# Attention decode, forward and backward: V transposed as fp32 pairs, and O by wide matmuls

## The chip, the cores and the metric

The kernel runs on one core of a Trainium2 chip. The metric is the device time of one execution in microseconds; smaller is better. The kernel before takes 668.13 us (median of three, 667.49 to 668.91). Its profiled execution spans 667.0 us.

## The reference

Softmax attention with one query row for each of 32 heads, 8192 keys and a head width of 128, all in bf16, and its gradients for a given gradient of the output:

```python
B, H, Sq, Skv, Dh = 1, 32, 1, 8192, 128

def _fwd_reference(q, k, v):
    scale = q.shape[-1] ** -0.5
    scores = jnp.einsum('bhqd,bhkd->bhqk', q, k) * scale
    attn = _softmax(scores, axis=-1)
    return jnp.einsum('bhqk,bhkd->bhqd', attn, v)

def reference(q, k, v, grad_out):
    ...
    _out, _vjp = jax.vjp(_f, q, k, v)
    _grads = _vjp(grad_out)
    return (_out0, *[jnp.asarray(_g) for _g in _grads])
```

With p the softmax row of a head and do its output gradient, a head needs o = p V; dp = V do; ds = p (dp - o·do) times the scale; dq = ds K; and the outer products dK = ds q and dV = p do. So K and V (2 MiB each) are read once per head, and dK and dV (2 MiB each) are written: 8.39 MB a head, 268 MB in all.

## The kernel before

A head's K or V lies in SBUF as [128 partitions, 64 slots, 128 columns]. The products o and dq contract over the keys, which lie in the partitions, so they take the tensor as it is. The scores of K and dp contract over the head width, so they need it transposed. K is transposed on VectorE in 32 x 32 blocks of fp32 words, each a pair of bf16. V is transposed on TensorE, 16 slots at a time, and copied out of PSUM by ScalarE:

```python
    def v_transposes(h, c):
        T_ps = psT.tile([P, CH, P], BF16, tag="T", name="T_ps")
        for i in range(CH):                                    # CH = 16
            nc.tensor.transpose(T_ps[:, i, :], Vt[h][:, c * CH + i, :], ident[:])   # L168
        X = tpool.tile([P, CH, P], BF16, tag="XT", name="XT_sb")
        nc.scalar.copy(X.rearrange("p c s -> p (c s)").bitcast(F32),                # L170
                       T_ps.rearrange("p c s -> p (c s)").bitcast(F32))
        XV[h, c] = X

    def v_scores(h, c):
        X = XV.pop((h, c))
        ...
        for i in range(CH):
            n = c * CH + i
            nc.tensor.matmul(st[h]["dp"][:, n:n + 1], lhsT=X[:, i, :], rhs=doT[:, h:h + 1],   # L180
                             start=True, stop=True, skip_group_check=True)

    def contract(Xt, rep, out_col, first=0, last=NT):          # NT = 64
        for n in range(first, last):
            nc.tensor.matmul(out_col, lhsT=Xt[:, n, :], rhs=rep[:, n, 0:1],                   # L185
                             start=(n == 0), stop=(n == NT - 1), skip_group_check=True)
```

`contract` makes the slot of K or V the stationary operand (128 columns loaded) and one column of weights the moving one. The loop runs one head's scores and softmax between the parts of the previous head's backward pass, in the order written (scheduling by the tool is off):

```python
    for h in range(H + 1):
        p_ = h - 1
        if h < H:
            for u in range(NCH):
                k_blocks(h, u)            # VectorE, L133: K transposed
            k_scores(h)                   # 64 matmuls of four columns, L145
            if 0 < h < H - 1:
                load_v(h + 1)             # L81
        if h > 0:
            ds_of(p_)                     # reads o.do through pdt, L216
            outer(p_, "dk", 0)            # VectorE, L195; its output leaves at L203
            dq_of(p_, 0)                  # contract over K
        ...                               # s_mask, s_swap: scores put into place, L161
        if h > 0:
            dq_of(p_, 1)
            outer(p_, "dk", 1)
        if 0 < h and h + 2 < H:
            load_k(h + 2)                 # L75
        ...                               # maximum (L255), q and do broadcast (L207), exp, sum (L268)
        x["p"] = small.tile([P, NT, R], BF16, tag="prep", name="p_rep")
        nc.scalar.activation(x["p"][:], ..., ACT.Copy, scale=rinv[:])       # R = 4 copies of p, L277
        ...
        v_transposes(h, 0)
        contract(Vt[h], x["p"], x["m"][:, 2:3])
        nc.scalar.copy(o_all[:, h:h + 1], x["m"][:, 2:3])
        v_transposes(h, 1)
        nc.tensor.matmul(x["m"][:, 1:2], lhsT=do_f[:, h:h + 1].to_broadcast([P, P]), rhs=o_all[:, h:h + 1],
                         start=True, stop=True, skip_group_check=True)      # o.do, L284
        v_scores(h, 0)
        v_transposes(h, 2)
        v_scores(h, 1)
        v_transposes(h, 3)
        v_scores(h, 2)
        v_scores(h, 3)
        outer(h, "dv", 0)
        ...                               # and 1, 2, 3
```

The stretch from `v_transposes(h, 0)` to `v_scores(h, 3)` is called the V phase of a head below. K has three buffers, V two, the transposed blocks in PSUM two.

## Time and profile before

| what | busy us | share of the span | a head (busy / 32) |
|---|---|---|---|
| PE, matmuls | 516.8 | 77% | 16.2 us |
| PEld, weight loads | 485.8 | 73% | 15.2 us |
| DVE (VectorE) | 512.5 | 77% | 16.0 us |
| ACT (ScalarE) | 182.1 | 27% | 5.7 us |
| main transfer queue | share of 16 engines' span | 97.0% | |

PE stands for TensorE. The four groups of PE that the change concerns or leaves beside it have these rows; the columns are the line, the engine and operation, the tiles, the count, then busy us and mean ns of one, then the idle time of the engine just before them:

```profile
L168 PE MATMUL T_ps<-ident,Vt 128*128 128x128 bf16 x2048 | 228.7, 302 | 31.9 <-DMA Vt<-in_v_dram 31.9
L180 PE MATMUL dp_ps<-doT,XT_sb 128*128 128x1 bf16 x2048 | 73.6, 166 | 24.4 <-ACT XT_sb L170 24.4
L185 PE MATMUL m_ps<-p_rep,Vt 128*128 128x1 bf16 x2048 | 60.5, 166 | 0.0
```

A mean is the duration of one matmul from start to end; consecutive ones overlap, so 16 transposes of 302 ns each need 1.73 us and not 4.8. Chains and timelines give the time of a whole block, and that is the number to work with.

### The profile page before, as it was taken

Reading aid. Unit: us, or ns where it says so; the run is one execution under the profiler, and the core shown is the slowest. Engines: PE = TensorE matmul, PEld = TensorE weight load, DVE = VectorE, ACT = ScalarE, POOL = GpSimd, SP = SyncE. Lnnn points to the kernel's source line nnn. Section 1 sums busy time; section 2 is a strip of 40 time slices with the busy share of each in tenths; the row PEclk is TensorE's granted clock in tenths of the full one; section 3 lists DMA queues with packets and bytes.
Section 4 is the critical chain, followed back from the end, with each engine's and each line's share of the span. In section 5 each row is a group of like instructions: output and inputs, shape, how many; then the busy total and the mean of one; then the engine's idle time right before and its main releaser. Section 6 shows DMA issues by size and latency. Waiting matters only on the chain.

```text
span 667.0 us, 23105 instructions
## 1 busy us (share of the span) xinstructions
PE 516.8 (77%) x10727; PEld 485.8 (73%) x10727; DVE 512.5 (77%) x658; ACT 182.1 (27%) x321; POOL 0.7 (0%) x6
## 2 busy tenths in 40 slices
PE   2887988888887777878779787787776888778881
PEld 1887878878877767877668676677766777677870
DVE  4797888888877797777877778777788776887762
ACT  0333323232323222232222322223312223223230
POOL 0000000000000000000000000000000000000000
PEclk9995556566565565555555655666557665555555
DMA  8999999999999999999999999999999999999783
GB/s 330 414 425 424 419 427 414 424 423 426 425 425 424 425 425 424 425 429 423 423 427 426 423 416 422 413 412 418 395 423 418 397 416 406 409 420 403 270 357 142
DMA packets 29807, 269.94 MB, mean 405 GB/s; under 512 B 3472, under 2 KB 3472, under 8 KB 6032
## 3 DMA queue, kind: packets, MB, share of 16 engines
q1 hardware_dynamic: 29712, 268.48, 97.0%
q8 instruction: 83, 1.36, 0.7%
q14 instruction: 12, 0.10, 0.0%
HBM read 134.23 MB, written 134.23 MB: 403 GB/s over the span
## 4 chain that ended last, share of the span: by engine, by line
DMA 75%; PE 17%; DVE 3%; ACT 2%; issue 1%; SPq 0%; ACTq 0%
DMA Kt<-in_k_dram 26%; DMA Vt<-in_v_dram 26%; DMA out_dram<-G_dv 23%; PE T_ps L168 7%; PE s_ps L145 2%; PE dp_ps L185 2%; PE m_ps L185 2%; PE dp_ps L180 1%; DVE XK_sb L133 1%; ACT XT_sb L170 1%; PE m_ps L255 1%; DVE G_dk L195 1%; PE m_ps L268 1%; PE s_ps L161 0%; ACT qd L211 0%
## 5 line engine op out<-in xcount | busy, mean ns | idle before, releaser
L168 PE MATMUL T_ps<-ident,Vt 128*128 128x128 bf16 x2048 | 228.7, 302 | 31.9 <-DMA Vt<-in_v_dram 31.9
L168 PEld LDWEIGHTS <-Vt 128*128 128x128 bf16 x2048 | 201.1, 142 | 33.8 <-DMA Vt<-in_v_dram 33.6
L133 DVE STREAM_TRANSPOSE XK_sb<-Kt 128x1024 f32<-128x1024 f32 x128 | 148.2, 1213 | 81.1 <-DMA Kt<-in_k_dram 81.1
L170 ACT COPY XT_sb<-T_ps 128x1024 f32<-128x1024 f32 x128 | 129.5, 1012 | 189.7 <-PE T_ps L168 189.7
L195 DVE TENSOR_TENSOR G_dk<-ds_rep,qd 128x2048 bf16<-128x2048 bf16 x128 | 155.7, 1219 | 1.1
L195 DVE TENSOR_TENSOR G_dv<-p_rep,qd 128x2048 bf16<-128x2048 bf16 x128 | 148.2, 1220 | 8.5 <-ACT p_rep L277 8.5
L180 PEld LDWEIGHTS <-XT_sb 128*128 128x128 bf16 x2048 | 74.7, 106 | 27.2 <-ACT XT_sb L170 27.2
L180 PE MATMUL dp_ps<-doT,XT_sb 128*128 128x1 bf16 x2048 | 73.6, 166 | 24.4 <-ACT XT_sb L170 24.4
L145 PE MATMUL s_ps<-q_blk,XK_sb 128*128 128x4 bf16 x2048 | 59.1, 168 | 23.2 <-DVE pdt L216 20.5
L145 PEld LDWEIGHTS <-XK_sb 128*128 128x128 bf16 x2048 | 56.5, 103 | 25.5 <-DVE pdt L216 22.3
L185 PE MATMUL dp_ps<-ds_rep,Kt 128*128 128x1 bf16 x2048 | 64.7, 165 | 6.6 <-issue 6.0
L185 PEld LDWEIGHTS <-Kt 128*128 128x128 bf16 x2048 | 59.9, 104 | 12.3 <-issue 12.3
L185 PEld LDWEIGHTS <-Vt 128*128 128x128 bf16 x2048 | 61.1, 105 | 0.0
L185 PE MATMUL m_ps<-p_rep,Vt 128*128 128x1 bf16 x2048 | 60.5, 166 | 0.0
L226 ACT COPY dq_all<-dp_ps 128x1 f32<-128x1 f32 x32 | 5.1, 159 | 173.9 <-PE dp_ps L185 173.9
L268 PEld LDWEIGHTS m_ps<-rs,ones_f 128*128 128x128 f32 x64 | 16.0, 310 | 48.6 <-ACT e L267 48.6
L268 PE MATMUL m_ps<-rs,ones_f 128*128 128x1 f32 x64 | 18.7, 360 | 39.2 <-ACT e L267 39.2
L264 DVE TENSOR_REDUCE nbias<-m_ps 128x1 f32<-128x128 f32 x32 | 9.3, 292 | 22.0 <-ACT qd L211 22.0
L255 PE MATMUL m_ps<-diag,ones_f 128*128 128x128 f32 x64 | 25.3, 499 | 0.7 <-DVE diag L253 0.7
L218 DVE SCALAR_TENSOR_TENSOR ds_rep<-dp_ps,pdt,p_s 128x256 bf16<-128x256 f32 x32 | 15.5, 484 | 12.0 <-PE dp_ps L180 9.6
L277 ACT ACTIVATE p_rep<-e,rinv 128x256 bf16<-128x256 f32 x32 | 16.2, 507 | 30.3 <-DVE rinv L275 30.3
L211 ACT CAST qd<-m_ps 128x256 bf16<-128x256 f32 x32 | 11.9, 372 | 42.4 <-PE m_ps L207 42.4
(40 smaller groups left out, 163.0 us busy)
## 6 DMA issues: line engine op xcount, KB each, us to landing
Kt<-in_k_dram SPq DMA_DIRECT2D x31, 2048.0 KB, 28.0
out_dram<-G_dv SPq DMA_DIRECT2D x62, 1024.0 KB, 25.8
out_dram<-G_dk SPq DMA_DIRECT2D x62, 1024.0 KB, 28.0
Vt<-in_v_dram SPq DMA_DIRECT2D x30, 2048.0 KB, 28.3
Vt<-in_v_dram SPq DMA_DIRECT2D x8, 512.0 KB, 13.8
Kt<-in_k_dram SPq DMA_DIRECT2D x4, 512.0 KB, 5.4
out_dram<-G_dv SPq DMA_DIRECT2D x4, 512.0 KB, 16.9
out_dram<-G_dk SPq DMA_DIRECT2D x4, 512.0 KB, 10.7
```

The source lines that it names most:

```text
L133: nc.vector.transpose(XK[h][:, :, :, u, :], slots(Kt[h], u, NCH).rearrange("p g d -> p (g d)").bitcast(F32).rearrange("p (g w j) -> p g w ...
L145: nc.tensor.matmul(out[:, g, :], lhsT=cols[:, g, c // 2, c % 2], rhs=q_blk[:, h, c, :], start=(c == 0), stop=(c == 2 * NB - 1), skip_group ...
L168: nc.tensor.transpose(T_ps[:, i, :], Vt[h][:, c * CH + i, :], ident[:])
L170: nc.scalar.copy(X.rearrange("p c s -> p (c s)").bitcast(F32), T_ps.rearrange("p c s -> p (c s)").bitcast(F32))
L180: nc.tensor.matmul(st[h]["dp"][:, n:n + 1], lhsT=X[:, i, :], rhs=doT[:, h:h + 1], start=True, stop=True, skip_group_check=True)
L185: nc.tensor.matmul(out_col, lhsT=Xt[:, n, :], rhs=rep[:, n, 0:1], start=(n == 0), stop=(n == NT - 1), skip_group_check=True)
L195: nc.vector.tensor_tensor(slots(G, r, 4).rearrange("p n (a b) -> p n a b", b=R), slots(rep, r, 4).unsqueeze(2).to_broadcast([P, Q, D // R, ...
L211: nc.scalar.copy(x["qd"][:].rearrange("p a d -> p (a d)"), x["m"][:, 256:512])
L218: nc.vector.scalar_tensor_tensor(out=x["ds"][:], in0=x["dp"][:, 0:NT].unsqueeze(2).to_broadcast([P, NT, R]), scalar=pdt[:], in1=x["p_s"][: ...
L255: nc.tensor.matmul(x["m"][:, 128:256], lhsT=ones_f[:], rhs=diag[:], start=True, stop=True, skip_group_check=True)
L268: nc.tensor.matmul(x["m"][:, 0:1], lhsT=ones_f[:], rhs=rs[:], start=True, stop=True, skip_group_check=True)
L277: nc.scalar.activation(x["p"][:], e[:].unsqueeze(2).to_broadcast([P, NT, R]), ACT.Copy, scale=rinv[:])
```

## The change

V is read as fp32 words, each a pair of neighbouring bf16 columns. A transpose of 128 words then covers two slots: 32 transposes a head in place of 64, with the same number of bytes in PSUM and in ScalarE's copy. After it, a partition holds the word column j of one slot (partitions 0 to 63) or of the next (64 to 127), and the two bf16 of a word stand side by side. `v_scores` takes them apart by stride: for each pair of slots two matmuls, for even and odd columns, accumulate into two output columns, with a weight `do_blk` that is zero for the other slot.

O no longer has V as the stationary operand. The weights of four slots (four columns) are stationary, and 512 columns of V (four slots) move past them: 16 matmuls for 64. Of the 4 x 512 result only the diagonal blocks (weights of slot b with columns of slot b) are wanted. ScalarE copies the result to SBUF, and four small fp32 matmuls with one-hot columns add the blocks up into a column. The wide matmuls stand in four groups between the other work of the V phase. The last head keeps the narrow contraction. The aim is to spare TensorE instructions and weight loads.

```diff
+    do_blk = consts.tile([P, H, 2, 2], BF16)
+    nc.vector.memset(do_blk[:], 0.0)
+    for e2 in range(2):
+        twice = consts.tile([H, 2, W], BF16, tag=f"twice{e2}")
+        ... (a copy, a transpose, and two copies into do_blk)
     def v_transposes(h, c):
-        T_ps = psT.tile([P, CH, P], BF16, tag="T", name="T_ps")
-        for i in range(CH):
-            nc.tensor.transpose(T_ps[:, i, :], Vt[h][:, c * CH + i, :], ident[:])
-        X = tpool.tile([P, CH, P], BF16, tag="XT", name="XT_sb")
-        nc.scalar.copy(X.rearrange("p c s -> p (c s)").bitcast(F32),
-                       T_ps.rearrange("p c s -> p (c s)").bitcast(F32))
+        T_ps = psT.tile([P, CH // 2, P], F32, tag="T", name="T_ps")
+        words = Vt[h].rearrange("p n d -> p (n d)").bitcast(F32)
+        for i in range(CH // 2):
+            m = c * CH // 2 + i
+            nc.tensor.transpose(T_ps[:, i, :], words[:, m * P:(m + 1) * P], ident_f[:])
+        X = tpool.tile([P, CH // 2, P], F32, tag="XT", name="XT_sb")
+        nc.scalar.copy(X[:], T_ps[:])
     def v_scores(h, c):
-        for i in range(CH):
-            n = c * CH + i
-            nc.tensor.matmul(st[h]["dp"][:, n:n + 1], lhsT=X[:, i, :], rhs=doT[:, h:h + 1],
-                             start=True, stop=True, skip_group_check=True)
+        X = XV.pop((h, c)).rearrange("p m s -> p (m s)").bitcast(BF16).rearrange("p (m s e) -> p m e s", s=P, e=2)
+        for i in range(CH // 2):
+            n = c * CH + 2 * i
+            for e2 in range(2):
+                nc.tensor.matmul(st[h]["dp"][:, n:n + 2], lhsT=X[:, i, e2, :], rhs=do_blk[:, h, e2, :],
+                                 start=(e2 == 0), stop=(e2 == 1), skip_group_check=True)
+    def contract_wide(Xt, rep, bank, first, last):
+        for g in range(first, last):
+            nc.tensor.matmul(bank[0:R, :], lhsT=rep[:, R * g:R * (g + 1), 0],
+                             rhs=Xt[:, R * g:R * (g + 1), :].rearrange("p n d -> p (n d)"),
+                             start=(g == 0), stop=(g == NT // R - 1), skip_group_check=True)
+    def gather_wide(bank, out_col):
+        four = small.tile([R, R, D], F32, tag="four", name="four")
+        nc.scalar.copy(four[:].rearrange("a b d -> a (b d)"), bank[0:R, :])
+        for b in range(R):
+            nc.tensor.matmul(out_col, lhsT=four[:, b, :], rhs=ident_f[0:R, b:b + 1],
+                             start=(b == 0), stop=(b == R - 1), skip_group_check=True)
 ... (the loop; broad = h < H - 1)
         v_transposes(h, 0)
-        contract(Vt[h], x["p"], x["m"][:, 2:3])
+        if broad:
+            contract_wide(Vt[h], x["p"], x["s"], 0, 4)
+        else:
+            contract(Vt[h], x["p"], x["m"][:, 2:3])
+        v_transposes(h, 1)
+        if broad:
+            contract_wide(Vt[h], x["p"], x["s"], 4, 8)
+        v_scores(h, 0)
+        v_transposes(h, 2)
+        if broad:
+            contract_wide(Vt[h], x["p"], x["s"], 8, 12)
+        v_scores(h, 1)
+        v_transposes(h, 3)
+        if broad:
+            contract_wide(Vt[h], x["p"], x["s"], 12, 16)
+            gather_wide(x["s"], x["m"][:, 2:3])
         nc.scalar.copy(o_all[:, h:h + 1], x["m"][:, 2:3])
-        v_transposes(h, 1)
+        v_scores(h, 2)
         nc.tensor.matmul(x["m"][:, 1:2], lhsT=do_f[:, h:h + 1].to_broadcast([P, P]), rhs=o_all[:, h:h + 1],
                          start=True, stop=True, skip_group_check=True)
-        v_scores(h, 0)
-        v_transposes(h, 2)
-        v_scores(h, 1)
-        v_transposes(h, 3)
-        v_scores(h, 2)
         v_scores(h, 3)
```

The result bank of the wide matmuls is the one that holds the head's scores, which are used up by then.

## The prediction

> **What bounds the kernel now.** I read four views, in this order: the page's slices, the DMA issues' own waits, the chain of waits, and one head in order of time. First the page's slices and its first queue, then what the queue that issues the transfers waited for:

> ```profile
> PEclk9995556566565565555555655666557665555555
> DMA  8999999999999999999999999999999999999783
> GB/s 330 414 425 424 419 427 414 424 423 426 425 425 424 425 425 424 425 429 423 423 427 426 423 416 422 413 412 418 395 423 418 397 416 406 409 420 403 270 357 142
> ...
> q1 hardware_dynamic: 29712, 268.48, 97.0%
> q8 instruction: 83, 1.36, 0.7%
> ```
> ```profile
> SPq L203 <- DMA out_dram<-G_dk: 111.7, 52, 2.5
> SPq L203 <- DMA Kt<-in_k_dram: 110.8, 26, 5.2
> SPq L75 <- DMA Vt<-in_v_dram: 97.5, 23, 4.5
> ```

> The transfer engines are full from the second slice to the 37th. A head moves 8.39 MB (four tensors of 2 MiB), which at 425 GB/s is 19.7 us; late in the run, at 406 to 413 GB/s, it is 20.5 us. The issue queue waits mostly for earlier transfers to land, not for an engine. So a gain on an engine buys nothing in the middle; a loss costs only once an engine needs more than about 20 us a head.

> The chain of waits puts 75% on DMA, but walks along PE at both ends. Start us, us, what, for one V phase of an early head and for the tail:

> ```profile
> 77.81 1.73 PE T_ps L168 x16
> 79.54 0.32 PE m_ps L284 x2
> 79.86 0.43 PE dp_ps L180 x16
> 80.29 1.54 PE T_ps L168 x16
> 81.82 0.38 PE dp_ps L180 x16
> 82.20 0.93 PE T_ps L168 x16
> ...
> 598.46 28.01 DMA Kt<-in_k_dram
> 626.50 4.62 DVE XK_sb L133 x4
> ```

> From the chain between 103.85 and 122.04 us, one head of PE work without a data wait is 18.2 us, against 19.7 to 20.5 us of transfers: PE has about 2 us to spare, no more. The same is seen in the middle of the run, where PE waits for V before the transposes and for DVE before the scores of K:

> ```profile
> 382.84 1.87 PE L145 MATMUL s_ps<-q_blk,XK_sb 128*128 128x4 bf16 x64 [1.35 <-DVE pdt L216]
> ...
> 391.24 1.89 PE L168 MATMUL T_ps<-ident,Vt 128*128 128x128 bf16 x16 [1.50 <-DMA Vt<-in_v_dram]
> 392.93 1.89 PE L185 MATMUL m_ps<-p_rep,Vt 128*128 128x1 bf16 x64
> ...
> 401.48 0.55 PE L180 MATMUL dp_ps<-doT,XT_sb 128*128 128x1 bf16 x16 [0.78 <-ACT XT_sb L170]
> ```

> These two waits (1.35 + 1.50 = 2.85 us of a 20.6 us head, in this stretch) are the whole room the change has. DVE (512.5 us over 32 heads, 16.0 us a head) and ACT (5.7 us) are further from the bound.

> [...] The trace has both for the transposes: 1.73 us for 16 is 108 ns, 0.93 us for 16 is 58 ns. It follows that the 1.0 printed for the granted clock in the first three slices is not to be believed, since blocks there also take 1.73 us. [...] No fp32 transpose runs in the kernel before, so this is the least certain number here.

> **The change, part by part.** Per head, gated / ungated, in us:

> 1. *Transposes.* 64 of bf16 become 32 of fp32 (each is one weight load and one matmul in the built program). Before: 4 blocks of 1.73 = 6.9. After: [...]4 blocks of 0.86 = 3.4 gated, 1.8 ungated. [...] For ordinary fp32 weight loads the trace has minima of 125 ns for 32 columns (L161) and 285 ns for 128 (L255): 160 ns over 96 columns, 1.67 ns each, or 213 ns for 128. If transposes load so, the blocks are 6.8 gated and 3.4 ungated: nothing saved.
> 2. *O.* 64 matmuls with one moving column took 1.69 in all. Now 16 with 512 columns[...]. This adds 5.1 or 1.8.
> 3. *Gather.* A copy of 512 elements on ACT: half the 1024-element copy (1.01 us), so about 0.55. It stands behind the fourth block's copy on ACT, and PE has nothing else in between: about 0.8 idle. Then four fp32 products; L284, the like, is two passes in 0.33, and four of them come to about 1.2. Together +2.0.
> 4. *Scores of V.* 64 matmuls with two moving columns in place of 64 with one: 26 ns each as before, no change. The 0.78 wait for the last ACT copy, which is before these, now lies under the gather: -0.8.
> 5. *Waiting for p.* The first wide group needs p right after one transposed block. Where PE waits for V, p is long there (390.55 against 391.24 us); else about 0.15.
> 6. *Off the path.* PE has 8,465 matmuls with their loads for 10,727[...]. The constants cost about 1 us more DVE at the start.

> The V phase took 11.5 us. Gated throughout, with cheap transposes, it is 11.5 - 3.5 + 5.1 + 2.0 - 0.8 + 0.15 = 14.5. Ungated throughout it is 11.5 - 5.1 + 1.8 + 2.0 - 0.8 = 9.4. I chose a mixture: [...]I expect the gate to lift some 5 us after it begins. The first two blocks and two wide groups (5.1 us) run gated and the rest ungated, which gives about 11.7. With dear transposes the same mixture is about 13.3. The head is then 18.4 to 20.0 us of PE, still not above the 20 us of transfers, so the middle does not move.

> The ends do. *Tail:* the last head keeps the narrow contraction but has the new transposes. Its V phase runs from 638.08 us with nothing else bounding it, and three of its four blocks are each up to 0.87 shorter, plus a little from the order: up to -3.8, with dear transposes 0. Head 30's longer V phase may push back the last scores of K by up to 1.3. I take -2.5. *Start:* +1 for the constants, and V of head 0 is released up to 2.6 us later, where the slices show transfers already short of work (380 GB/s from 25 to 30 us): +1.5 in all. *Program:* -0.7. The sum is 668.1 - 2.5 + 1.5 - 0.7 = 666.4 us.

> **The rivals.**

> *PE becomes the bound.* If the gate stays down, a head is 18.2 + 3.0 = 21.2 us with cheap transposes (some +1 us on most of 31 heads, about 690 us), and 24.6 with dear ones (about 790). For it: the granted clock is 0.5 to 0.6 over most of the run, and the gate lifts before only now and then. Against it: a late PE stops waiting for V[...]. [...]

> *A real gain.* If the late dips in bandwidth (395 and 397 GB/s) came from PE's fetches or from jitter on PE, fewer instructions could bring the middle to 425: about 200 us x 3% = 6 us; with the tail, 657. I see no sign that PE causes them: the engines are full in these slices too. Over 2% (654.8) is hardly in reach.

> *Order of buffers.* Transfers are issued far ahead (28 us from issue to landing, over a head's worth), so V released a microsecond or two later should not empty the queue, except at the start.

> **Range and chances.** Centre 666.5. The low end, 657, is the tail's whole gain plus the bandwidth rival. The high end, 690, is the gated PE with cheap transposes. Faster by over 2% 0.07; within 2% 0.72; slower by over 2% (above 681.5) 0.21, nearly all of it from PE as the bound.

> **What would show it.** Right: DMA slices still at 9 with about 425 GB/s; [...]PE still waiting for V. Transposes: a block of eight at 0.86 or below (cheap) or at 1.7 gated (dear). Tail: the time from the last landing of K to the end falls from 40.5 us (667.0 - 626.5) to 37 or 38. Wrong: slices of DMA at 8 or lower with the chain on PE throughout, PE above 20 us a head, or bandwidth changed at full engines.

## The result: 690.3 us, 3.4% slower

The changed kernel takes 690.3 us (689.72 to 692.38), the kernel before 668.09; the ratio is 1.0337, 95% interval 1.0313 to 1.0361. The profiled execution spans 688.4 us against 667.0.

The page of the changed kernel (slices, the instruction queue, the chain's shares):

```profile
PEclk9977677767777777777777777777777777777775
DMA  8999999999999999999999999999999999999945
GB/s 337 418 414 410 414 386 374 378 396 398 389 396 423 408 410 424 408 404 412 396 413 418 407 414 379 367 396 405 397 380 377 428 425 419 409 391 422 409 194 225
...
q8 instruction: 66, 1.08, 0.6%
...
PE 81%; ACT 11%; issue 4%; DVE 3%; DMA 1%; SPq 0%; ACTq 0%
```

The last line for the kernel before:

```profile
DMA 75%; PE 17%; DVE 3%; ACT 2%; issue 1%; SPq 0%; ACTq 0%
```

The chain was 75% DMA and is now 81% PE and 1% DMA. The transfer engines' share still prints 9 in all but the first and the last two slices, but what they moved fell to 367 to 398 GB/s in many: the share counts the time of packets, so here the bytes tell and the share does not. The waits of the issue queue say the same. Its longest were for landings; now (total us, times, longest us) they are for engines:

```profile
SPq L229 <- DVE mx L277: 159.8, 27, 11.3
SPq L229 <- DVE G_dv L221: 157.3, 66, 13.5
SPq L81 <- PE s_ps L203: 145.8, 30, 5.6
```

One head of the changed kernel along the chain (start us, us, what):

```profile
332.29 1.81 PE T_ps L180 x8
334.10 1.80 PE s_ps L203 x4
335.89 1.65 PE T_ps L180 x8
337.55 0.96 PE s_ps L203 x4
338.50 0.49 PE dp_ps L192 x16
338.99 0.93 PE T_ps L180 x8
339.92 0.96 PE s_ps L203 x4
...
343.40 0.48 ACT four L209
343.88 0.04 issue
343.92 1.05 PE m_ps L211 x8
...
346.07 1.61 PE s_ps L154 x64
```

Gated stands for a granted clock of 0.50 and ungated for 1.00: the trace has 0.50 from 332.29 to 335.89 us, 1.00 from 338.99 to 340.88, and the gate is said to lift where the one becomes the other (337.16). Eight fp32 transposes take 1.81 us gated and 0.93 ungated, what sixteen bf16 ones took (1.73 and 0.93): per transpose twice as long. Four wide matmuls take 1.80 gated and 0.96 ungated, 4.7 us a head for the 1.7 us of the narrow contraction. The gather is 1.05 us of products behind a copy on ACT. From the first transposes to the next scores of K the V phase is 13.8 us (332.29 to 346.07) where it was 11.5 in a head before that waits for no data:

```profile
110.54 1.73 PE T_ps L168 x16
...
122.04 1.71 PE s_ps L145 x64
```

*Where the 21.4 us are.* From the first to the last scores of K there are 31 heads. Before: 12.37 to 631.18 us, 19.96 a head. After: 13.69 to 660.11, 20.85 a head, so 31 x 0.89 = +27.6. The start is 1.3 later. After the last scores of K the end comes in 28.3 us instead of 35.8, -7.5: the last outer product to the end of the span is 4.5 us (683.95 to 688.4) instead of 12.3 (654.73 to 667.0), as the output queue is no longer deep (a transfer of dK lands 9.7 us after its issue in the median, 28.0 before). Sum: +21.4.

### The profile page after: what moved, and what is told of

Read it like the earlier page. It is cut to its first block, busy times and chain, and to the rows that moved or that the text cites. A ratio compares the mean times of both kernels' runs of the same rounds, so it can differ in the third digit from the quotient of the medians.

```text
span 688.4 us, 18684 instructions
## 1 busy us (share of the span) xinstructions
PE 589.3 (86%) x8465; PEld 424.8 (62%) x8465; DVE 513.5 (75%) x664; ACT 196.6 (29%) x352; POOL 0.7 (0%) x6
## 3 DMA queue, kind: packets, MB, share of 16 engines
q1 hardware_dynamic: 29712, 268.48, 97.0%
q8 instruction: 66, 1.08, 0.6%
## 4 chain that ended last, share of the span: by engine, by line
PE 81%; ACT 11%; issue 4%; DVE 3%; DMA 1%; SPq 0%; ACTq 0%
PE T_ps L180 24%; PE s_ps L203 17%; PE dp_ps L192 9%; PE dp_ps L197 8%; PE s_ps L154 8%; PE m_ps L211 5%; ACT XT_sb L182 5%; PE m_ps L281 3%; PE m_ps L294 3%; ACT four L209 2%; ACT e L293 2%; PE s_ps L170 2%; ACT qd L237 2%; PE m_ps L233 2%; DVE nbias L290 1%
## 5 line engine op out<-in xcount | busy, mean ns | idle before, releaser
L180 PE MATMUL T_ps<-ident_f,Vt 128*128 128x128 f32 x1024 | 182.1, 336 | 0.0
L180 PEld LDWEIGHTS T_ps<-ident_f,Vt 128*128 128x128 f32 x1024 | 153.6, 181 | 25.6 <-issue 25.6
L203 PE MATMUL s_ps<-Vt,p_rep 128*4 128x512 bf16 x496 | 152.8, 439 | 0.0
L192 PEld LDWEIGHTS <-XT_sb 128*128 128x128 bf16 x2048 | 63.5, 98 | 27.7 <-issue 26.2
L242 DVE COPY pdt<-m_ps 128x1 f32<-128x1 f32 x32 | 5.1, 158 | 99.9 <-PE m_ps L326 99.9
L203 PEld LDWEIGHTS <-p_rep 128*4 128x4 bf16 x496 | 34.8, 90 | 69.5 <-issue 45.5
L197 PEld LDWEIGHTS <-Kt 128*128 128x128 bf16 x2048 | 60.2, 104 | 21.6 <-issue 21.2
L192 PE MATMUL dp_ps<-do_blk,XT_sb 128*128 128x2 bf16 x2048 | 70.5, 164 | 0.0
L154 PE MATMUL s_ps<-q_blk,XK_sb 128*128 128x4 bf16 x2048 | 56.8, 167 | 2.7 <-DVE XK_sb L142 2.7
L211 PEld LDWEIGHTS m_ps<-ident_f,four 4*128 4x128 f32 x248 | 29.9, 186 | 36.4 <-ACT four L209 36.4
L211 PE MATMUL m_ps<-ident_f,four 4*128 4x1 f32 x248 | 32.5, 248 | 20.7 <-ACT four L209 20.7
## 6 DMA issues: line engine op xcount, KB each, us to landing
Vt<-in_v_dram SPq DMA_DIRECT2D x30, 2048.0 KB, 11.7
```

Source lines behind the costliest of these rows:

```text
L154: nc.tensor.matmul(out[:, g, :], lhsT=cols[:, g, c // 2, c % 2], rhs=q_blk[:, h, c, :], start=(c == 0), stop=(c == 2 * NB - 1), skip_group ...
L180: nc.tensor.transpose(T_ps[:, i, :], words[:, m * P:(m + 1) * P], ident_f[:])
L192: nc.tensor.matmul(st[h]["dp"][:, n:n + 2], lhsT=X[:, i, e2, :], rhs=do_blk[:, h, e2, :], start=(e2 == 0), stop=(e2 == 1), skip_group_chec ...
L203: nc.tensor.matmul(bank[0:R, :], lhsT=rep[:, R * g:R * (g + 1), 0], rhs=Xt[:, R * g:R * (g + 1), :].rearrange("p n d -> p (n d)"), start=( ...
L211: nc.tensor.matmul(out_col, lhsT=four[:, b, :], rhs=ident_f[0:R, b:b + 1], start=(b == 0), stop=(b == R - 1), skip_group_check=True)
```

## The experiments

Theory A: PE sets the pace, because the wide matmuls and the gather lengthen the V phase and the transposes give nothing back. Theory B: the fp32 transposes are to blame. Theory C: the transfers became slower by themselves.

| run | us | ratio to before | 95% |
|---|---|---|---|
| e1 pairs, narrow O | 663.9 | 0.9933 | 0.9915 to 0.9950 |
| e2 bf16 transposes, wide O | 677.6 | 1.0134 | 1.0104 to 1.0164 |
| e3 no gather | 663.3 | 0.9927 | 0.9912 to 0.9942 |
| e4 gather twice | 718.4 | 1.0759 | 1.0737 to 1.0781 |
| e5 order only | 667.8 | 0.9998 | 0.9990 to 1.0007 |
| e6 gather hidden | 663.2 | 0.9922 | 0.9906 to 0.9938 |
| e7 gather in bf16 | 662.1 | 0.9918 | 0.9897 to 0.9940 |
| e8 e1, last V whole | 662.9 | 0.9925 | 0.9911 to 0.9938 |
| e9 e1, padded | 665.8 | 0.9966 | 0.9953 to 0.9980 |
| e10 e6, last V whole | 661.7 | 0.9900 | 0.9885 to 0.9916 |
| e11 512 instructions a head | 676.9 | 1.0131 | 1.0114 to 1.0148 |
| e12 e11, one wide more | 677.0 | 1.0135 | 1.0122 to 1.0149 |
| e13 before, half of dp | 663.7 | 0.9937 | 0.9923 to 0.9950 |

### e1: the pairs alone

```diff
-        broad = h < H - 1
+        broad = False
```

> The changed kernel with the narrow contraction of O in every head: V still transposed as fp32 pairs, no wide matmuls, no gather. Theory A (PE is the bound, because the wide matmuls and the gather lengthen the V phase, while a block of eight fp32 transposes costs what sixteen bf16 ones did, 1.81 against 1.73 us): a head of PE is back at about 18.3 us, below the transfers, so 666 to 672 us. Theory B (the fp32 transposes are to blame): it stays at 683 to 692 us. Theory C (transfers themselves became slower, 374 to 397 GB/s at full engines, whatever PE does): no lower than 680 us.

663.9 us, 26 less than the changed kernel, below the kernel before and 2 us below the range of A. B falls. The transposes are as slow here (1.81 us gated), but a head of PE still fits under the transfers.

### e2: the wide contraction alone

```diff
-        T_ps = psT.tile([P, CH // 2, P], F32, tag="T", name="T_ps")
-        ... (eight fp32 transposes; two-column scores with do_blk)
+        T_ps = psT.tile([P, CH, P], BF16, tag="T", name="T_ps")
+        ... (sixteen bf16 transposes; one-column scores with doT, as before)
```

> The changed kernel with V transposed and dp computed as before (64 bf16 transposes, one-column scores), O still by wide matmuls with the gather. Theory A: blocks of 1.73 us gated and 0.93 ungated for 1.81 and 1.03 shorten the head by about 0.4 us, so 676 to 690 us, far from the time before. Theory B: 666 to 672 us.

677.6 us: within A's range. Of the 22 us that the change costs, 13 go when the bf16 transposes come back (a head is 20.58 us in the mean for 20.85, and the scores of K begin 1.4 us earlier), yet the pairs cost nothing on their own (e1). Both follow if a head of PE is above the transfers with the wide contraction and below them without.

### e3 and e4: the gather out, and twice

```diff
-            gather_wide(x["s"], x["m"][:, 2:3])
-        nc.scalar.copy(o_all[:, h:h + 1], x["m"][:, 2:3])
+            nc.scalar.copy(o_all[:, h:h + 1], x["s"][:, 2:3])      # e3: O is left out
```
```diff
             gather_wide(x["s"], x["m"][:, 2:3])
+            gather_again(x["m"][:, 3:4])                           # e4: the same four products
```

> The changed kernel without the gather in heads 0 to 30 (no ACT copy of the 4 x 512 result, no four fp32 products; O is read from an arbitrary column instead, so O and what depends on it are left out of the computation). All wide matmuls and fp32 transposes stay. Theory A: 0.67 us of wait and 1.05 us of products go, the head falls from 20.85 to about 19.1 us of PE and is under the transfers' 19.96: 664 to 674 us. Theory C: the transfers are the same, so 686 us or more.

> The changed kernel with the four fp32 products of the gather done a second time into an unused column (1.0 us more PE a head, nothing else). Theory A: PE sets the pace, so 31 x 1.0 us more: 715 to 725 us. Theory C, or any bound beside PE: within 4 us of 690.

663.3 and 718.4 us. The second gather costs 28.1 us over 31 heads, 0.91 each: PE time passes nearly whole to the end. Without the gather 1.7 us of PE go, and with all 496 wide matmuls and 1,024 fp32 transposes in place the time is below that of before. Its chain, by engine, is back with the transfers:

```profile
DMA 63%; PE 26%; DVE 7%; ACT 1%; issue 1%; SPq 0%; ACTq 0%
```

A holds, C falls. But e3 takes away more than the gather's work. With eight matmuls and their loads fewer its head is 512 instructions of PE instead of 528, and the stops of PE that cost the changed kernel 17.4 us (see e11) are gone from its trace too. e11 has 512 instructions with the gather in place and takes 676.9 us, so about half of the 27 us between the changed kernel and e3 is the gather's and the rest went with the stops.

### e6 and e7: the same work, the wait hidden

```diff
         v_scores(h, 0)
+        if broad:
+            contract_wide(Vt[h], x["p"], x["s"], 8, 16)
+            four = gather_copy(x["s"])             # ACT copies while PE transposes
         v_transposes(h, 2)
         v_scores(h, 1)
         v_transposes(h, 3)
+        if broad:
+            gather_wide(four, x["m"][:, 2:3])
```
```diff
-        four = small.tile([R, R, D], F32, tag="four", name="four")
+        four = small.tile([R, R, D], BF16, tag="four", name="four")    # e7, on top of e6
```

> The changed kernel with the same work in another order: all wide matmuls before the third block of transposes, the ACT copy of their result right after them, and the four fp32 products after the fourth block, so that PE does not wait for the copy (0.67 us a head in the changed kernel). Theory A: 31 x 0.67 = 21 us less than 690, 667 to 675 us. Theory C: no change.

> The same as e6 with the copied result rounded to bf16, so that the gather is four one-pass products, about 0.15 us for 1.0. Theory A: PE falls to some 19.3 us a head, below the transfers, and the time stops at the floor that two runs have shown: 662 to 666 us, in spite of the 496 wide matmuls.

e6 takes 663.2 us, better than the 667 to 675 expected; the wait of PE for the copy (20.7 us in all) is gone, the stops are 12.5 us for 17.4, and the V phase is 12.7 us in the mean for 13.6. e7 takes 662.1; the intervals overlap, so the cheaper products (0.25 us for four in bf16, 1.05 in fp32, by the timelines) bring nothing that can be told. With the hole behind the copy filled, the wide contraction is below both kernels, but it gains nothing over the narrow one (e1, 663.9, overlapping intervals), and PE stays nearly as long as the transfers: a head of e6 is 19.84 us in the mean, and its chain is still

```profile
PE 79%; DVE 8%; DMA 5%; ACT 4%; issue 3%; SPq 0%; ACTq 0%
```

### e5, e9, e13: why e1 is below the kernel before

e5 is e2 with `broad = False`: the kernel before in the changed order. e9 and e13:

```diff
         v_scores(h, 3)
+        for _ in range(32):                        # e9, on top of e1
+            nc.tensor.matmul(x["m"][:, 4:5], lhsT=ident[:], rhs=ident[:, 0:1], ...)
```
```diff
-        for i in range(CH):                        # e13, on the kernel before
+        for i in range(0, CH, 2):                  # half of dp is left out
             n = c * CH + i
-            nc.tensor.matmul(st[h]["dp"][:, n:n + 1], lhsT=X[:, i, :], rhs=doT[:, h:h + 1], ...)
+            nc.tensor.matmul(st[h]["dp"][:, n:n + 2], lhsT=X[:, i, :], rhs=doT[:, h:h + 1].to_broadcast([P, 2]), ...)
```

> The kernel before with only the changed kernel's order of the V phase (V score blocks and the product o.do one place later); bf16 transposes, narrow contraction. It asks why the fp32 pairs with the narrow contraction took 663.9 us, 4 us less than before. If the order did it: 662 to 665 us. If the pairs did it (960 fewer matmuls with their loads[...]): 667 to 669 us.

> The fp32 pairs with the narrow contraction (663.9 us) and 32 useless one-column matmuls a head into an unused column, so that TensorE runs as many instructions as in the kernel before (10,729 matmuls against 10,727). If the 4 us come from the smaller program, they go again: 667 to 669 us. If they come from the pairs themselves: 663 to 665 us, as the padding of 0.85 us a head fits under the transfers.

> The kernel before with 32 of the 64 score matmuls of V a head, each writing two columns (half of dp is left out): as few matmuls as with the fp32 pairs and the narrow contraction, but bf16 transposes. If the 4 us of the pairs come from the smaller program or less TensorE time: 663 to 665 us. If from the pairs themselves: 667 to 669 us.

The order does nothing (0.9998). With bf16 transposes and 32 fewer matmuls a head the time is 663.7, as with the pairs; so it is not the pairs as such but the smaller program or the PE time (by the pages e1 has 1,022 matmuls fewer than the kernel before, not 960). The padded pairs fell between the two forecasts (665.8) and do not tell these two apart: the padding also brings PE into the chain (51%, in e1 23%), and PE stops before the products of dq, with nothing the profile shows to wait for, 17.5 us in all (6.3 in e1). The page shows the gain as bandwidth late in the run: the slices from the 25th to the 33rd are 395 to 423 GB/s before, and 413 to 427 in e1. Why fewer small matmuls do that at full engines stays open.

### e8 and e10: the last head's V in one transfer

```diff
-        parts = NCH if h in (0, H - 1) else 1
+        parts = NCH if h == 0 else 1
```

> The fp32 pairs with the narrow contraction, and the last head's V loaded in one transfer instead of four. If the end is held up by the issue queue, which spends 10.7 us on these four (from 611 us in the kernel before), 657 to 662 us; if the end is set by the last head's work on the engines, 663 to 665 us as with four.

> The wide contraction with the hidden gather (e6, 663.2 us) and the last head's V in one transfer. With the narrow contraction the latter brought 0 to 1 us; the same here: 662 to 664 us.

662.9 and 661.7 us, each 1.0 to 1.5 below its partner, with intervals that overlap; e8 lies at the edge of its second forecast, so no hold-up by the issue queue is shown. e10 is the lowest time found, 1.0% below the kernel before, with the wide contraction and the gather in fp32; e7 and e8 are not told apart from it.

### e11 and e12: the stops, and what was left

In the changed kernel's chain PE stands still in 12 heads for 0.9 to 2.1 us, 17.4 us together, with nothing the profile shows to wait for. The matmuls after such stops (x is how many of the block were still to come):

```profile
58.04 0.18 PE L197 MATMUL dp_ps<-ds_rep,Kt 128*128 128x1 bf16 x1 [1.20 <-issue]
79.32 0.40 PE L197 MATMUL dp_ps<-ds_rep,Kt 128*128 128x1 bf16 x9 [1.74 <-issue]
101.55 0.61 PE L197 MATMUL dp_ps<-ds_rep,Kt 128*128 128x1 bf16 x17 [1.71 <-issue]
...
392.08 0.19 PE L197 MATMUL dp_ps<-ds_rep,Kt 128*128 128x1 bf16 x1 [1.29 <-issue]
413.88 0.40 PE L197 MATMUL dp_ps<-ds_rep,Kt 128*128 128x1 bf16 x9 [2.09 <-issue]
```

Each stop stands 8 matmuls with their loads, 16 instructions, ahead of the last one, and 16 heads later the series returns (58.04 and 392.08 us). So the place repeats every 16 x 16 = 256 instructions, an estimate from these moves. It fits the 528 instructions that a head of PE has in the built program, 2 x 256 + 16. In e4, with 544, the stops of neighbouring heads are 16 matmuls apart (32 instructions), which fits too:

```profile
212.30 0.98 PE L198 MATMUL dp_ps<-ds_rep,Kt 128*128 128x1 bf16 x31
214.62 0.19 PE L198 MATMUL dp_ps<-ds_rep,Kt 128*128 128x1 bf16 x1 [1.33 <-issue]
235.09 0.56 PE L198 MATMUL dp_ps<-ds_rep,Kt 128*128 128x1 bf16 x15
237.91 0.61 PE L198 MATMUL dp_ps<-ds_rep,Kt 128*128 128x1 bf16 x17 [2.27 <-issue]
```

So e11 makes the head 512 instructions, which should keep the place where it is from head to head:

```diff
-            for c in range(2 * NB):
+            last = 2 * NB - 1 - g % 2              # 8 of 64 score matmuls of K are left out
+            for c in range(last + 1):
                 nc.tensor.matmul(out[:, g, :], ..., start=(c == 0), stop=(c == last), skip_group_check=True)
```

> The changed kernel with 8 of the 64 score matmuls of K left out in each head (a part of the scores is left out), so that TensorE's program is 512 instructions a head instead of 528. In the changed kernel PE stood still for 0.9 to 2.1 us in 12 heads, each time 16 instructions earlier in the head than in the head before, and from the 16th head on the same again: as if the program came in blocks of 256 instructions. If so, the block's edge now stays at one place, which by counting back is in the second block of transposes and in the scores of K, where none of the 12 stood: no such stops, 17 us less, and 6 us less for the 8 matmuls, 665 to 673 us. If the stops have another cause, only the 8 matmuls count: 682 to 687 us.

676.9 us. The stops are gone (the longest "issue" left in the chain is 0.34 us), but only 13.4 of the expected 17 to 25 us came. The 8 matmuls left out (0.21 us a head) brought nothing, because PE now waits as long for VectorE (6.4 us over 31 heads, 0.7 in the changed kernel):

```profile
341.95 0.80 PE L282 MATMUL m_ps<-diag,ones_f 128*128 128x128 f32 x2 [0.20 <-DVE diag L280]
```

```diff
-            last = 2 * NB - 1 - g % 2
+            last = 2 * NB - 1 - (g % 2 or g == 0)            # a ninth one left out
-        for g in range(first, last):
+        for g in [0] * (first == 0) + list(range(first, last)):   # the first wide matmul twice
```

> The run with 512 instructions a head (676.9 us), a ninth score matmul of K left out and the first wide matmul of a head done twice: the same number of instructions, 0.45 us more of gated TensorE work a head, less 0.03 (a part of the scores is left out). In that run and in quiet stretches of the changed kernel the head takes 20.48 us[...]. [...]the added work is paid back by an earlier ungating of the second block of transposes (now 1.72 us, 1.03 ungated) and the head stays at 20.48: 675 to 679 us. If the head is the sum of its work, 31 x 0.42 = 13 us more: 688 to 692 us.

677.0 us: the added matmul costs nothing. Along the chain, e11 and then e12:

```profile
324.40 1.81 PE T_ps L181 x8
326.21 1.80 PE s_ps L204 x4
328.01 1.65 PE T_ps L181 x8
```
```profile
305.76 1.81 PE T_ps L181 x8
307.57 2.23 PE s_ps L204 x5
309.80 1.23 PE T_ps L181 x8
```

The five wide matmuls take 0.43 us more, and the transposes after them 0.42 less: by the 1.81 and 0.93 us of a whole block the gate lifts 0.4 to 0.5 us earlier in the phase (an estimate). In the changed kernel's quiet heads it lifts at 296.20, 316.68 and 337.16 us, 20.48 apart. My reading is that a head that comes late to the next step of the grid is gated for less time, one that comes early for more, so that the period settles on six steps. The first heads of e11 fit this: from the second on they take 20.00, 20.24, 20.35, 20.42, 20.45 and 20.47 us, so the distance to 20.48 about halves from head to head, as is to be expected where work runs at half speed (1.81 us a block for 0.93) up to a fixed time. In both runs PE waits for no transfer after the first head, so the transfers do not set this period. Even without the lock, the second copy would have cost less than the 13 us I wrote: with the gate lifting at a fixed place in the phase it moves 0.24 us of ungated work (0.96 / 4), 7 us in all, an estimate. The measured 0.2 us is far from either.

## Why the prediction failed, step by step

**The bound (missed, the step that failed).** The step is "18.4 to 20.0 us of PE, still not above the 20 us of transfers, so the middle does not move". Measured, a quiet head takes PE 20.48 us, with a V phase of 13.8 us for my 11.7 to 13.3; the stops bring the mean to 20.85; and the transfers need at most the 19.8 of e1 and e3. So PE is above the transfers by 1 us a head. The centre took cheap transposes, and they were dear. For dear ones "about 13.3" does not follow from the mixture as written: 11.5 with transposes 5.1 for 6.9, the wide matmuls +3.4 (between the 5.1 and 1.8 that I had estimated), gather +2.0 and the wait -0.8 is 14.3, a head of 21.0. With the gate lifting after 5 us, one wide group sooner, as the trace has it, the same terms give 13.5, a head of 20.2. Either way the terms put PE above 20 us, and the rival that I gave 0.21 was the sum of my own terms. "Still not above" is worth little with up to 20.0 us against 20.

**Transposes.** The dear case was right: 226 ns gated (1.81 / 8) and 116 ungated (0.93 / 8), twice a bf16 one (108 and 58). I had built the centre on the cheap case; that an fp32 transpose takes no longer than a bf16 one was my assumption, and the runs show twice the time.

**O.** 450 ns gated (1.80 / 4) and 240 ungated (0.96 / 4). Four times the 108 and 58 ns of a bf16 transpose of 128 columns, which the trace before shows, is 432 and 232 (an estimate). The group of O takes 4.7 us a head, 3.0 more than the narrow form, for the +3.4 of the mixture, as the gate lifted one wide group sooner.

**Gather.** 0.67 us of wait and 1.05 of products, 1.7 for 2.0. The old wait of 0.78 went, as said.

**The gate.** It lifts 4.9 us into the V phase (332.29 to 337.16), near the 5 chosen, and it does so after a stretch of which 3.1 us are transposes. What makes it lift was not shown. What was not in the prediction is that a head can settle on a whole number of steps of 3.413 us.

**The stops.** Not in the prediction: 17.4 us in the chain. They were in the trace before too (five of over 0.6 us, 5.6 us together, the longest 1.99 us up to 52.93). Two of them, among the early heads, stand on its chain; later the chain is the transfers'.

**The tail.** The direction was right, the size and the reason wrong. -2.5 was to come from cheaper transposes in the last head; its V phase was no shorter (12.1 us, before 11.6). -7.5 came from the output queue, which this PE-bound run kept short (9.7 us from issue to landing of dK for 28.0).

**The start** (+1.5) was +1.3. The -0.7 for the program was my estimate and is not shown on its own; the instruction queue moves 1.08 MB for 1.36. The rival of lost bandwidth was half right: e1, e3 and e13, with fewer matmuls, move more GB/s late in the run and take 4 to 5 us less than the kernel before; that the number of matmuls is the cause is not shown.

## What to carry to other kernels

A loop bound by transfers with 2 us of room on an engine is one sum away from being bound by that engine: add up the whole engine time of an iteration, both from gated and from ungated block times, and distrust a result as close to the other bound as the 20.0 us here (20.48 measured, 19.8 for the transfers). Swapping the operands of a matrix-vector product trades weight loads for streamed columns; here 64 narrow matmuls took 1.7 us and 16 wide ones 4.7, and even with the copy behind it out of the engine's way the swap brought nothing over the narrow form (663.2 us and 663.9).

## What the runs showed that was not expected

- **Stops that move with the instruction count.** PE stands still for 0.9 to 2.1 us in 12 heads of the changed kernel, ten times among the products of dq (26 ns for a matmul with its load) and twice at L170. The place moves by the head's instruction count modulo 256, the estimate from e11: by 16 a head in the changed kernel, by 32 in e4, not at all in e11 and e3, where the stops vanish. The instruction queue fits: 66 packets for 2 x 8,465 instructions are 257 to a packet, an estimate from the page. What PE waits for at these places is in no view.
- **A loop locked to a grid of the clock.** In the changed kernel, e11 and e12 the head settles on 20.48 us, six of the steps of 3.413 us on which the clock of the changed kernel and of the kernel before changes, and the 0.42 us of work added in e12 change nothing. That the grid sets the period is inferred from these times. In e6 the times of the heads repeat over three of them, 17 steps being 58.03 us (first transposes of a head; the two lines are three heads apart):

```profile
576.90 1.81 PE T_ps L180 x8
...
634.93 1.81 PE T_ps L180 x8
```
